# One core: single up products and wide gate pairs in an S4 convolution beside a gated GLU

## The chip, the cores and the metric

One Trainium2 chip, one of its cores. The metric is the device time of one execution in microseconds, lower is better; several runs of each kernel are compared by their medians. TensorE is written PE, VectorE DVE, ScalarE ACT, GpSimd POOL and SyncE SP, as the profile does.

## The reference

The input `A_u` has 2048 tokens of 512 features. It is layer-normalised, and two branches work on the result. The outcome is the input plus both.

```python
x = A_u
xn = _layernorm(x, axis=-1)
# branch A: a diagonal state space model as a long causal convolution, one kernel per feature
P = jnp.exp(logdA[:, :, None] * l[None, None, :])            # logdA = exp(log_dt) * (A_re + 1j A_im), 512 x 128 modes
K = jnp.einsum("dn,dnl,dn->dl", Cc, P, dB).real              # 512 features x 2048 lags
y = irfft(rfft(xn padded) * rfft(K padded))[:L] + xn * Dskip
# branch B: a gated unit with 1792 hidden features
g = xn @ w_gate;  u = xn @ w_up
h = _sigmoid(g) * u
return x + y + h @ w_down
```

## The kernel before, in words

**The parts.** Tokens are loaded (`load_x`, L437) and normalised: statistics L542 and L543, a power on POOL (L492 or L482), normalising L554 (DVE) or L549 (ACT). The first 512 tokens are transposed on PE through `ident` (L565) and copied to `xnT` in two halves, the first by ACT (L572), the second by DVE (L574); the other three groups of 512 tokens go through memory (`x_scr`) and a transposing DMA.

Branch A builds the modes' powers by squaring (L610 to L678), then, for four quarters `c` of 128 features each, two tables G and H by complex products on DVE (`cmul`, L737 to L743, and `squares`, L791 to L797). PE multiplies the tables (`f_k`, L822, 64 small matmuls for each half) to kernel matrices, ACT evicts them to `kq_sb` (L288), they are stored to memory in two pieces (`k_scr`) and reloaded into `kT`; L844 on DVE adds Dskip. Two quarters make one half `pc` of the features. For each half, eight units `u` make the kernel's spectrum on PE (L911), the input's spectrum (L695 to z_scr, then L885), their product on DVE (L916, L920; L898 are copies that swap halves for it) and the way back on PE (L935). Results go through `v_scr` and are reloaded for the last step (L994, L997).

Branch B runs over four groups `grp` of 512 tokens, in each over 14 hidden tiles `k` of 128, taken as seven pairs `u2`. A gate product is four matmuls 128x512 (`fg`, L1045), a sigmoid on ACT puts it into `hT_sb` (L1057, or L1060 for a pair at once), an up product is four matmuls (`fu`, L1069), and DVE multiplies the two. Then the down product (L1123) takes 14 matmuls for each 128 tokens, and ACT evicts it.

**PSUM.** Two pairs of banks (`pair`, pool `s`, 1024 wide) and four single banks (`bank`, pool `gu`). A gate product stands in a single bank; if its pair is listed in `JOINT`, both gate products of the pair stand in one pair of banks and one sigmoid takes 1024 columns.

**Up products.** `UEV` lists the products (number 14 grp + k) whose up part ACT evicts to `us_sb` (L1084). In the kernel before they come in pairs: two evictions fill one of two wide buffers, and one DVE instruction multiplies 128x1024 (L1089). `FLIP` lists the pairs whose second eviction goes first. The other up products are multiplied straight from PSUM, 128x512 (L1094).

**The start of the first group.** For k in `HALF` the gate product is done by halves of its columns, so that it can begin when half of `xnT` is there. Before that PE runs matmuls on a zeroed tile (`keep_warm`, L519).

**The reload of the kernel matrices.** For every quarter two stores and one load of 192 KB; the very last store is issued by ACT, all others by SP.

**What sets the order.** `_Plan.add` records operations in the order of the code; `run` issues them by the list `ORDER`, a written-out permutation of their numbers, and hands out pool slots in that order. Every engine works through its instructions in the order issued, and a DMA waits in its engine's queue until what it needs is done. So one list fixes the order on all five engines, DMAs included.

Of the kernel before, what the change touches and what calls it, by code (L numbers as in the profile page):

```python
# [10 lines left out]
BF = mybir.dt.bfloat16  # L11
# [14 lines left out]
FT = 14  # L26
# [21 lines left out]
FLIP = ((0, 3), (0, 5), (1, 0), (1, 1), (1, 2), (1, 4), (1, 5), (1, 6), (2, 0), (2, 4), (3, 2))  # L48
JOINT = ((0, 2), (0, 3), (0, 5), (0, 6))
# [18 lines left out]
KB = 1024  # L68
# [114 lines left out]
def _consts():  # L183
# [19 lines left out]
UEV = (6, 7, 10, 11, 12, 13, 14, 15, 16, 17, 18, 19, 22, 23, 24, 25, 26, 27, 28, 29, 30, 31, 32, 33, 34, 35, 36, 37, 38, 39, 40, 41, 44, 45, 46, 47, 52, 53, 54, 55,)  # L203
# [115 lines left out]
def kernel(  # L319
# [46 lines left out]
    us_sb = const.tile([128, 2, 2, 512], BF, name="us_sb")  # L366
# [77 lines left out]
    load_x(2, 1)  # L444
    load_x(3, 1)
# [76 lines left out]
    keep_warm(12, -10)  # L522
    for n in (0, 5, 6):
        keep_warm(3 if n < 3 else 1, -9 + n)
# [196 lines left out]
    k_ld = []  # L721
# [27 lines left out]
    for c in range(4):  # L749
# [63 lines left out]
        for half_ in range(2):  # L813
            sl = _Slot("s")

            def f_k(half_=half_, sl=sl, G=G, H=H):
                for y in range(8 * half_, 8 * half_ + 8):
                    pk = bank(sl, y // 4 % 2).rearrange("p (q x) -> p q x", q=4)
                    for comp in range(2):
# [13 lines left out]
        kq_free = [dma("ACT" if cc and c in (3,) else "SP", k_scr[4 * c:4 * c + 4, :, :, cc, :].rearrange("t i h x -> (t i) h x"),  # L833
                       kq[cc:128:2, cc:16:2].rearrange("p h k y -> p h (k y)"), deps=evs, prio=PC, pkt=192)(96 * KB) for cc in range(2)]
        k_st[pc] += kq_free
        half_kT = slice(4 * (c % 2), 4 * (c % 2) + 4)
        k_ld.append(dma("SP", kT[pc][:, half_kT].rearrange("p a c k y -> p a (c k y)"), k_scr[4 * c:4 * c + 4].rearrange("a i h c x -> (i h) a (c x)"),
                        deps=kq_free + W_op + [o_g], prio=PC, pkt=384)(192 * KB))
        if c % 2 == 0:
            continue  # L840

# [3 lines left out]
        kT_op[pc] = [pl.add("DVE", 0.30, f_ds, k_ld[-2:] + [l_dk], PC)]  # L845
# [179 lines left out]
    for grp in range(4):  # L1025
# [5 lines left out]
        for u2 in range(7):  # L1031
# [4 lines left out]
            for k in (2 * u2, 2 * u2 + 1):  # L1036
# [38 lines left out]
                un = FT * grp + k  # L1075
                on = un in UEV

                if on:
                    if k % 2 == 0:
                        eu0, es0 = (b, mu, k), es_  # L1080
                        continue
                    eus, us = [], _Slot("us")
                    for n, (sl, m_, kk) in enumerate([(b, mu, k), eu0] if (grp, u2) in FLIP else [eu0, (b, mu, k)]):
                        eus.append(pl.add("ACT", 0.48, lambda sl=sl, us=us, kk=kk: S.activation(out=us_sb[:, us.idx, kk % 2, :], in_=bank(sl), func=ACT.Identity),  # L1084
                                          [m_] + eus, PSIG, acq=[] if n else [us], rel=[sl], alt=(FT * grp + kk, 1)))

                    def fpd2(hs=hs, us=us):
                        hh = hT_sb[:, hs.idx, :, :].rearrange("p k n -> p (k n)")
                        V.tensor_tensor(out=hh, in0=hh, in1=us_sb[:, us.idx, :, :].rearrange("p k n -> p (k n)"), op=ALU.mult)  # L1089
                    prods.append(pl.add("DVE", 0.33, fpd2, [es0, es_] + eus, PPROD, rel=[us], alt=(un, 2)))  # L1090
                    continue

                def fpd(sl=b, h=h):
                    V.tensor_tensor(out=h(), in0=h(), in1=bank(sl), op=ALU.mult)  # L1094
                tail = dict(rel=[b], alt=(un, 2))
# [117 lines left out]
```

## Time and profile before

| | |
|---|---|
| median of 3 runs | 215.45 us (214.41, 215.45, 215.57) |
| the profiled execution | 215.32 us |
| its span, first to last instruction | 213.4 us |
| granted PE clock, mean | 0.997 |
| DMA moved | 42.61 MB, mean 200 GB/s |

A row of the timeline gives start, length, engine, line, operation, output and inputs, shape, how many in a row, and in brackets the idle time before and what ended it. "q" behind an engine is its sequencer, which issues DMAs. A window row gives the stretch and its length, then busy time and number of instructions on PE, PE's weight loads, DVE, ACT and POOL, the granted PE clock, the DMA engines' busy share and GB/s. Instructions overlap a little with the next one: the distance of two starts is what an instruction costs its engine, its length is more.

### The profile page before, as it was taken

The numbers are of one execution on the slowest core, as the hardware profiler recorded it, in microseconds if no ns is written. First come the engines' busy times: TensorE is split into PE (matmuls) and PEld (weight loads), VectorE is DVE, ScalarE is ACT, GpSimd is POOL, SyncE is SP. The second block draws the span as 40 slices with busy tenths as digits, with TensorE's granted clock in tenths as the row PEclk, the third lists the DMA queues.
The fourth block names the chain that finished last, engine by engine and source line by source line (L and its number), as shares of the span: only waits on it lengthen the run. The fifth ranks groups of instructions, "written<-read, shape, count | busy, mean of one in ns | idle before, by whom it ended". The sixth has DMA issues, their size and how long they took to land.

```text
span 213.4 us, 4897 instructions
## 1 busy us (share of the span) xinstructions
PE 204.0 (96%) x1839; PEld 103.2 (48%) x1864; DVE 191.3 (90%) x406; ACT 176.3 (83%) x284; POOL 33.1 (15%) x40
## 2 busy tenths in 40 slices
PE   7989999999999999999999999999999999999892
PEld 2654444444444454345447464444644655644472
DVE  4799999999999999999999999999973999990494
ACT  4799999999999999998998999779979699960000
POOL 2108030003040000010009970011200000000000
PEclk9999999999999999999999999999999999999998
DMA  5998597013963218788776369589994789897955
GB/s 148 330 372 313 182 225 237 2 52 133 260 139 60 98 55 263 185 238 212 215 216 159 112 174 275 141 231 244 175 257 112 203 252 335 246 288 209 263 195 178
DMA packets 52377, 42.61 MB, mean 200 GB/s; under 512 B 16641, under 2 KB 44546, under 8 KB 52354
## 3 DMA queue, kind: packets, MB, share of 16 engines
q1 hardware_dynamic: 50658, 40.30, 64.3%
q0 software_dynamic: 864, 1.57, 4.8%
q10 hardware_dynamic: 832, 0.43, 0.8%
q8 instruction: 14, 0.23, 0.4%
q14 instruction: 9, 0.07, 0.1%
HBM read 24.99 MB, written 12.85 MB: 177 GB/s over the span
## 4 chain that ended last, share of the span: by engine, by line
PE 59%; ACT 20%; DMA 9%; DVE 6%; issue 4%; POOL 1%; DVEq 0%; ACTq 0%; SPq 0%
PE bank L1069 15%; PE bank L1123 13%; PE bank L1045 11%; PE pair L911 9%; ACT big L288 6%; PE pair L935 5%; ACT hT_sb L1057 3%; PE pair L1045 3%; DMA k_scr<-kq_sb 3%; ACT us_sb L1084 3%; ACT big L669 3%; ACT big L663 2%; DVE big L1020 2%; DMA big<-v_scr 2%; PE pair L822 2%
## 5 line engine op out<-in xcount | busy, mean ns | idle before, releaser
L288 ACT ACTIVATE big<-pair 128x1024 bf16<-128x1024 f32 x64 | 64.6, 1048 | 5.3 <-PE pair L911 2.2
L1069 PE MATMUL bank<-xnT,wu_sb 128*128 128x512 bf16 x212 | 53.0, 379 | 1.1 <-issue 0.6
L1123 PE MATMUL bank<-wd_sb,hT_sb 128*128 128x512 bf16 (+1 forms) x231 | 50.6, 367 | 0.5 <-issue 0.2
L1045 PE MATMUL bank<-xnT,wg_sb 128*128 128x512 bf16 (+1 forms) x194 | 46.6, 370 | 0.5 <-issue 0.3
L1045 PEld LDWEIGHTS <-wg_sb 128*128 128x128 bf16 x240 | 22.7, 98 | 25.8 <-issue 3.0
L1123 PEld LDWEIGHTS <-hT_sb 128*128 128x128 bf16 x238 | 22.4, 98 | 24.9 <-issue 1.9
L1069 PEld LDWEIGHTS <-wu_sb 128*128 128x128 bf16 x224 | 20.7, 98 | 25.5 <-issue 3.4
L1057 ACT ACTIVATE hT_sb<-bank 128x512 bf16<-128x512 f32 x48 | 28.7, 640 | 2.3 <-PE bank L1045 2.3
L737 DVE TENSOR_TENSOR big<-big 128x1024 bf16<-128x1024 bf16 (+4 forms) x40 | 26.8, 670 | 0.2
L738 DVE TENSOR_TENSOR big<-big 128x1024 bf16<-128x1024 bf16 (+4 forms) x40 | 26.6, 666 | 0.0
L1084 ACT ACTIVATE us_sb<-bank 128x512 bf16<-128x512 f32 x40 | 24.7, 640 | 0.0
L911 PE MATMUL pair<-big 128*128 128x256 bf16 x160 | 19.4, 273 | 0.4 <-DVE big L844 0.4
L916 DVE TENSOR_TENSOR big<-big 128x2048 bf16<-128x2048 bf16 x16 | 19.3, 1219 | 0.1
L846 POOL COPY hold<-big 1x1 bf16<-1x1 bf16 x2 | 14.3, 7146 | 30.7 <-DVE big L844 30.7
L911 PEld LDWEIGHTS <-big 128*128 128x128 bf16 x160 | 15.3, 98 | 4.8 <-issue 1.0
L742 DVE TENSOR_TENSOR big<-big 128x512 bf16<-128x512 bf16 (+4 forms) x40 | 16.6, 415 | 0.3
L743 DVE TENSOR_TENSOR big<-big 128x512 bf16<-128x512 bf16 (+4 forms) x40 | 16.6, 414 | 0.0
L791 ACT ACTIVATE sq_sb<-big 128x256 bf16<-128x256 bf16 (+2 forms) x20 | 14.0, 698 | 1.3 <-DVE big L743 1.0
L935 PE MATMUL pair<-big 64*64 64x512 bf16 (+1 forms) x256 | 13.1, 327 | 0.5 <-ACT big L288 0.3
L1089 DVE TENSOR_TENSOR hT_sb<-hT_sb,us_sb 128x1024 bf16<-128x1024 bf16 x20 | 13.5, 684 | 0.0
L288 ACT ACTIVATE big<-big 128x256 bf16<-128x256 bf16 x30 | 13.1, 463 | 0.0
L669 ACT ACTIVATE big<-big 128x1024 f32<-128x1024 f32 x11 | 12.4, 1125 | 0.4 <-DVE big L678 0.4
(100 smaller groups left out, 233.4 us busy)
## 6 DMA issues: line engine op xcount, KB each, us to landing
big<-c_E SPq DMA_DIRECT2D x13, 320.0 KB, 5.1
z_scr<-big SPq DMA_DIRECT2D x16, 256.0 KB, 3.0
big<-z_scr SPq DMA_DIRECT2D x16, 256.0 KB, 3.9
v_scr<-big SPq DMA_DIRECT2D x16, 256.0 KB, 4.1
big<-big SPq DMA_DIRECT2D x44, 64.0 KB, 3.3
big<-in_A_u_dram SPq DMA_DIRECT2D x4, 512.0 KB, 6.7
wu_sb<-in_B_w_up_dram SPq DMA_DIRECT2D x2, 896.0 KB, 10.6
wd_sb<-in_B_w_down_dram SPq DMA_DIRECT2D x1, 1792.0 KB, 8.3
```

What stands on the lines that cost most here:

```text
L288: nc.scalar.activation(out=get(out), in_=get(in_), func=ACT.Identity)
L669: s_op = pl.add("ACT", 0.95, lambda cur=cur, sq=sq: S.activation(out=sq, in_=cur, func=ACT.Square), [cur_op] + W_op[-1:], PLAD + k * 0.01)
L737: V.tensor_tensor(out=wide(outp), in0=wide(lo), in1=mre, op=ALU.mult)
L738: V.tensor_tensor(out=wide(tb()), in0=wide(lo), in1=mim, op=ALU.mult)
L911: T.matmul(two(sk)[:, o:o + DW], es()[:, g, kt, :], kTv[p][:, :, kt, :], start=kt in (0, NKT - 1), stop=kt >= NKT - 2)
L916: V.tensor_tensor(out=pp().rearrange("p q h m -> p (q h) m"), in0=xx().rearrange("p q h m -> p (q h) m"), in1=kb()[:, 0:2 * DW].unsqueeze( ...
L935: T.matmul(two(sv)[o:o + 64, DW * (2 * g + y):2 * DW * (g + 1)], mab[b:b + 64, 2 * u + g, q, :], pq()[b:b + 64, q, ch] if y else pp()[b:b ...
L1045: T.matmul(bank(sl, k % 2)[:, c0:c1], w[:, kt, k * 128:(k + 1) * 128], xnT[:, grp, kt, c0:c1], start=(kt == 0), stop=(kt == KT - 1))
L1057: S.activation(out=hT_sb[:, hs.idx, k % 2, :], in_=bank(sl), func=ACT.Sigmoid)
L1069: T.matmul(bank(sl), wu_sb[:, kt, k * 128:(k + 1) * 128], xnT[:, grp, kt, :], start=(kt == 0), stop=(kt == KT - 1))
L1084: eus.append(pl.add("ACT", 0.48, lambda sl=sl, us=us, kk=kk: S.activation(out=us_sb[:, us.idx, kk % 2, :], in_=bank(sl), func=ACT.Identity ...
L1123: T.matmul(bank(po)[:, 0:c[1] - c[0]], hT_sb[:, hts[k // 2].idx, k % 2, jj * 128:(jj + 1) * 128], wd_sb[:, k, c[0]:c[1]], start=first and ...
```

## The change

- Three pairs of the third group, (2, 1), (2, 3) and (2, 5), join `JOINT`.
- `us_sb` holds single products: two buffers of 512 columns instead of two of 1024. Every product is evicted and multiplied by itself, 128x512. `FLIP` goes. `UEV` lists 40 products, as before, but not the same ones.
- Tokens are loaded as 1, 1, 2 (then 4, 4, 4) instead of 1, 1, 1, 1.
- The reload of the kernel matrices is done once for two quarters, 384 KB, behind all four stores. The last store is issued by SP.
- One more warming call, and 14 instead of 12 matmuls in the first: 22 instead of 17.
- The buffer for POOL's DMA descriptors has the default size.
- `ORDER` is another permutation throughout, since operations are fewer and more: 932 before, 963 after.

```diff
-FLIP = ((0, 3), (0, 5), (1, 0), (1, 1), (1, 2), (1, 4), (1, 5), (1, 6), (2, 0), (2, 4), (3, 2))
-JOINT = ((0, 2), (0, 3), (0, 5), (0, 6))
+JOINT = ((0, 2), (0, 3), (0, 5), (0, 6), (2, 1), (2, 3), (2, 5))
...
-    us_sb = const.tile([128, 2, 2, 512], BF, name="us_sb")
+    us_sb = const.tile([128, 2, 512], BF, name="us_sb")
...
-    load_x(2, 1)
-    load_x(3, 1)
+    load_x(2, 2)
...
-    keep_warm(12, -10)
-    for n in (0, 5, 6):
+    keep_warm(14, -10)
+    for n in (0, 1, 5, 6):
...
-        kq_free = [dma("ACT" if cc and c in (3,) else "SP", k_scr[4 * c:4 * c + 4, :, :, cc, :].rearrange("t i h x -> (t i) h x"),
+        kq_free = [dma("SP", k_scr[4 * c:4 * c + 4, :, :, cc, :].rearrange("t i h x -> (t i) h x"),
...
-        k_ld.append(dma("SP", kT[pc][:, half_kT].rearrange("p a c k y -> p a (c k y)"), k_scr[4 * c:4 * c + 4].rearrange("a i h c x -> (i h) a (c x)"),
-                        deps=kq_free + W_op + [o_g], prio=PC, pkt=384)(192 * KB))
         if c % 2 == 0:
             continue
+        kr = dma("SP", kT[pc].rearrange("p a c k y -> p a (c k y)"), k_scr[8 * pc:8 * pc + 8].rearrange("a i h c x -> (i h) a (c x)"),
+                 deps=k_st[pc] + W_op + [o_g], prio=PC, pkt=384)(384 * KB)
...
-                if on:
-                    if k % 2 == 0:
-                        eu0, es0 = (b, mu, k), es_
-                        continue
...
-                    def fpd2(hs=hs, us=us):
-                        hh = hT_sb[:, hs.idx, :, :].rearrange("p k n -> p (k n)")
-                        V.tensor_tensor(out=hh, in0=hh, in1=us_sb[:, us.idx, :, :].rearrange("p k n -> p (k n)"), op=ALU.mult)
-                    prods.append(pl.add("DVE", 0.33, fpd2, [es0, es_] + eus, PPROD, rel=[us], alt=(un, 2)))
...
+                def feu(sl=b, us=us, on=on):
+                    if on:
+                        S.activation(out=us_sb[:, us.idx, :], in_=bank(sl), func=ACT.Identity)
+                eu = pl.add("ACT", 0.48, feu, [mu], PSIG, acq=[us] if on else [], rel=[b] if on else [], alt=(un, 1))
+
+                def fpd(sl=b, h=h, us=us, on=on):
+                    V.tensor_tensor(out=h(), in0=h(), in1=us_sb[:, us.idx, :] if on else bank(sl), op=ALU.mult)
...
-    nc = _bacc.Bacc("TRN2", target_bir_lowering=False, num_devices=1, dynamic_dma_scratch_size=8192)
+    nc = _bacc.Bacc("TRN2", target_bir_lowering=False, num_devices=1)
```

Two engines in two places, each first before and then in the change. Lines after the changed places have other numbers there: L1083 for L1089 and L1094, L842 for L844, L741 for L742 and so on.

DVE at the start, before, from the statistics of tokens 2 and 3 on (`ln_ve_b`) to the copy into `xnT` and the next statistics:

```order
9 L486 TENSOR_SCALAR ln_ve_b<-mvb 128x2
10 L489 CAST ln_m_f<-mvb 128x2
11 L493 RECIPROCAL ln_ri_f<-ln_sd_b 128x2
12 L554 TENSOR_SCALAR big<-big,ln_m_f,ln_ri_f 128x512 x2
13 L610 TENSOR_TENSOR big<-big 128x512 x2
14 L618 TENSOR_SCALAR big<-big 128x512
15 L619 SCALAR_TENSOR_TENSOR big<-big 128x512
16 L574 COPY xnT<-pair_64 128x4x256
17 L542 BN_STATS stats<-big 128x6 x4
```

DVE in the same place in the change:

```order
10 L610 TENSOR_TENSOR big<-big 128x512
11 L489 CAST ln_m_f<-mvb 128x2
12 L610 TENSOR_TENSOR big<-big 128x512
13 L493 RECIPROCAL ln_ri_f<-ln_sd_b 128x2
14 L554 TENSOR_SCALAR big<-big,ln_m_f,ln_ri_f 128x512
15 L618 TENSOR_SCALAR big<-big 128x512
16 L619 SCALAR_TENSOR_TENSOR big<-big 128x512
17 L554 TENSOR_SCALAR big<-big,ln_m_f,ln_ri_f 128x512
18 L542 BN_STATS stats<-big 128x6 x2
19 L574 COPY xnT<-pair_64 128x4x256
20 L542 BN_STATS stats<-big 128x6
```

Both L610 moved ahead of the normalising of tokens 2 and 3 (L554), which is split, and the first two statistics of tokens 4 to 7 moved ahead of the copy L574.

SP around the last quarter's kernel matrices, before (`big<-big` are the swaps, `big<-z_scr` loads of input spectra, `v_scr` stores of results; the second store of this quarter is in ACT's queue):

```order
73 L422 DMA big<-z_scr 128x4x256
74 L422 DMA big<-big 32x1024
75 L422 DMA big<-z_scr 128x4x256
76 L422 DMA k_scr<-kq_sb 512x1x96
77 L422 DMA big<-c_S 128x128
78 L422 DMA big<-c_SR 128x256
79 L422 DMA big<-big 32x1024 x4
80 L422 DMA big<-k_scr 128x4x192
```

SP in the same place in the change:

```order
74 L423 DMA v_scr_99<-big 128x4x256
75 L423 DMA big<-big 32x1024
76 L423 DMA v_scr_99<-big 128x4x256
77 L423 DMA big<-c_S 128x128
78 L423 DMA k_scr<-kq_sb 512x1x96 x2
79 L423 DMA big<-z_scr 128x4x256
80 L423 DMA big<-big 32x1024 x3
81 L423 DMA big<-k_scr 128x8x192
```

Both stores stand in SP's queue. Of the two z_scr loads ahead of them one has moved behind them and the other to before these rows, with two v_scr stores in between. One swap fewer stands ahead of the reload, and the reload is twice as large.

More of the change, by code (lines that the diff above doesn't have):

```diff
@@ L201, in _consts @@
                 MAB=f(np.stack([quads(MA[by], True), quads(MB[by], True)], axis=2)), E=f(_build_E(M2, by).reshape(128, NU // 2, 2, NKT, 128).transpose(1, 0, 2, 3, 4)))
-UEV = (6, 7, 10, 11, 12, 13, 14, 15, 16, 17, 18, 19, 22, 23, 24, 25, 26, 27, 28, 29, 30, 31, 32, 33, 34, 35, 36, 37, 38, 39, 40, 41, 44, 45, 46, 47, 52, 53, 54, 55,)
+UEV = (0, 6, 7, 9, 11, 12, 13, 14, 15, 16, 17, 18, 19, 21, 23, 24, 25, 26, 28, 29, 30, 31, 32, 33, 34, 35, 36, 37, 38, 39, 40, 41, 43, 44, 46, 47, 49, 52, 54, 55,)
 ON_DVE = (86, 89, 104, 106, 121, 122, 123, 137, 138, 184, 194, 195, 198, 199, 201,)
@@ L720 @@
     kT_op = [[], []]
-    k_ld = []
     k_st = [[], []]
@@ L832 @@
         pc = c // 2
-        kq_free = [dma("ACT" if cc and c in (3,) else "SP", k_scr[4 * c:4 * c + 4, :, :, cc, :].rearrange("t i h x -> (t i) h x"),
+        kq_free = [dma("SP", k_scr[4 * c:4 * c + 4, :, :, cc, :].rearrange("t i h x -> (t i) h x"),
                        kq[cc:128:2, cc:16:2].rearrange("p h k y -> p h (k y)"), deps=evs, prio=PC, pkt=192)(96 * KB) for cc in range(2)]
         k_st[pc] += kq_free
-        half_kT = slice(4 * (c % 2), 4 * (c % 2) + 4)
-        k_ld.append(dma("SP", kT[pc][:, half_kT].rearrange("p a c k y -> p a (c k y)"), k_scr[4 * c:4 * c + 4].rearrange("a i h c x -> (i h) a (c x)"),
-                        deps=kq_free + W_op + [o_g], prio=PC, pkt=384)(192 * KB))
         if c % 2 == 0:
             continue
+        kr = dma("SP", kT[pc].rearrange("p a c k y -> p a (c k y)"), k_scr[8 * pc:8 * pc + 8].rearrange("a i h c x -> (i h) a (c x)"),
+                 deps=k_st[pc] + W_op + [o_g], prio=PC, pkt=384)(384 * KB)
         def f_ds(pc=pc):
@@ L844, in f_ds @@
             V.tensor_tensor(out=kz, in0=kz, in1=dskr[0:1, DW * pc:DW * pc + DW].rearrange("p (a y) -> p a y", y=16), op=ALU.add)
-        kT_op[pc] = [pl.add("DVE", 0.30, f_ds, k_ld[-2:] + [l_dk], PC)]
+        kT_op[pc] = [pl.add("DVE", 0.30, f_ds, [kr, l_dk], PC)]
         pl.add("POOL", 0.1, lambda pc=pc: P.tensor_copy(out=hold[:, pc:pc + 1], in_=kTv[pc][0:1, 0, 0, 0:1]), kT_op[pc], PC)
@@ L1075 @@
                 un = FT * grp + k
+                us = _Slot("us")
                 on = un in UEV
-                if on:
-                    if k % 2 == 0:
-                        eu0, es0 = (b, mu, k), es_
-                        continue
[L1082 to L1085, printed above, removed]
-                    def fpd2(hs=hs, us=us):
-                        hh = hT_sb[:, hs.idx, :, :].rearrange("p k n -> p (k n)")
-                        V.tensor_tensor(out=hh, in0=hh, in1=us_sb[:, us.idx, :, :].rearrange("p k n -> p (k n)"), op=ALU.mult)
-                    prods.append(pl.add("DVE", 0.33, fpd2, [es0, es_] + eus, PPROD, rel=[us], alt=(un, 2)))
[L1091 to L1095, printed above, removed]
+                def feu(sl=b, us=us, on=on):
[4 more added lines that the diff above has]
+                    V.tensor_tensor(out=h(), in0=h(), in1=us_sb[:, us.idx, :] if on else bank(sl), op=ALU.mult)
+                tail = dict(rel=[us] if on else [b], alt=(un, 2))
                 if joint and k % 2 == 0:
-                    held = fpd, [mu], tail
+                    held = fpd, [eu, mu], tail
                     continue
@@ L1100 @@
                     prods.append(pl.add("DVE", 0.33, held[0], held[1] + [es_], PPROD, **held[2]))
-                prods.append(pl.add("DVE", 0.33, fpd, [es_, mu], PPROD, **tail))
+                prods.append(pl.add("DVE", 0.33, fpd, [es_, eu, mu], PPROD, **tail))
         ges = []
```

82 rows, old and new, of the table ORDER are left out of this document.

## Prediction

> **What bounds the kernel now.** I read the page first, for the engines' shares, then the windows by stage, then the timeline where one stage hands over to the next.
>
> ```profile
> PE 204.0 (96%) x1839; PEld 103.2 (48%) x1864; DVE 191.3 (90%) x406; ACT 176.3 (83%) x284; POOL 33.1 (15%) x40
> ```
>
> Three engines are nearly full, so a share alone does not say which one sets the end. The windows do; each row gives the stretch, its length, then busy time by engine:
>
> ```profile
> 0.00:11.70 11.70, 9.45 (x49) 5.00 (x50) 7.40 (x22) 7.36 (x13) 2.32 (x11) 1.00 0.80 252
> 11.70:78.00 66.30, 65.88 (x345) 29.50 (x354) 66.04 (x156) 65.77 (x111) 11.41 (x16) 1.00 0.56 165
> 78.00:154.00 76.00, 75.05 (x850) 38.45 (x860) 75.43 (x163) 70.43 (x122) 18.90 (x12) 1.00 0.75 197
> 154.00:165.80 11.80, 10.83 (x207) 5.25 (x208) 6.72 (x12) 10.47 (x14) 0.00 (x0) 1.00 0.73 188
> 165.80:191.00 25.20, 24.75 (x252) 14.40 (x256) 24.82 (x43) 21.38 (x27) 0.43 (x1) 1.00 0.89 264
> 191.00:213.40 22.40, 18.00 (x143) 10.56 (x143) 10.85 (x14) 0.90 (x2) 0.00 (x0) 0.97 0.71 217
> ```
>
> From 11.7 to 154 VectorE rests 0.83 us in all and TensorE 1.37 us. Both are bounds, at the full granted clock (1.00): VectorE makes the long-convolution kernel's factors, TensorE fills the time with gate, up and down products. From 154 to 165.8 VectorE is busy for 6.72 of 11.80 us. That is the handover: the last quarter of the kernel matrices goes through memory.
>
> ```profile
> 154.02 1.40 PEld L822 LDWEIGHTS <-big 128*32 128x32 bf16 x128 [0.42 <-DVE big L743]
> 154.03 1.53 PE L822 MATMUL pair<-big 128*32 128x82 bf16 x128
> 155.02 1.51 ACT L288 ACTIVATE kq_sb<-pair 128x768 bf16<-128x768 f32 x2 [0.53 <-PE pair L822]
> 156.56 0.64 ACTq L422 DMA_DIRECT2D k_scr<-kq_sb  x1
> 156.63 0.57 SPq L422 DMA_DIRECT2D k_scr<-kq_sb  x1
> 158.44 3.68 SPq L422 DMA_DIRECT2D big<-big  x4
> 162.74 0.38 SPq L422 DMA_DIRECT2D big<-k_scr  x1
> 165.49 0.28 DVE L844 TENSOR_TENSOR big<-big,dskr 1x256 bf16<-1x256 bf16 x1 [0.51 <-DMA big<-k_scr]
> 165.82 2.36 PE L911 MATMUL pair<-big 128*128 128x256 bf16 x20 [0.35 <-DVE big L844]
> ```
>
> The last kernel matmuls (L822, 154.03) wait for VectorE's last factor; their result is evicted, stored, reloaded, corrected by L844, and the second half's spectra (L911) start at 165.82. What starts later there ends later, because TensorE is busy for 24.75 of the next 25.20 us.
>
> **The change part by part.** The sum is made against the profiled execution: 215.32 us, its span 213.4; the median of the runs is 215.45.
>
> *Products one by one.* 20 wide products, 128x1024, become 40 of 128x512. Four of the narrow form on VectorE run from the first row below to the start of the second; two wide ones follow them:
>
> ```profile
> 52.16 0.41 DVE L742 TENSOR_TENSOR big<-big 128x512 bf16<-128x512 bf16 x1
> ...
> 53.51 1.21 DVE L737 TENSOR_TENSOR big<-big 128x2048 bf16<-128x2048 bf16 x1
> ...
> 189.28 1.29 DVE L1089 TENSOR_TENSOR hT_sb<-hT_sb,us_sb 128x1024 bf16<-128x1024 bf16 x2
> 190.48 1.88 DVE L1094 TENSOR_TENSOR hT_sb<-hT_sb,bank 128x512 bf16<-128x512 bf16 x3
> ```
>
> A narrow one steps in 1.35/4 = 0.34 us, a wide one in 1.20/2 = 0.60. A pair costs 2 x 0.3375 - 0.60 = 0.075 more. Ahead of the last kernel factor the old order has 16 wide products and the new 32 narrow ones, with the same other work (ten products straight from PSUM in both). So VectorE gets 16 x 0.075 = 1.2 us more there; with whole durations instead of steps (2 x 0.41 - 0.645) it would be 2.8, the upper bound. The four remaining pairs cost 0.3 after 154, beside its idle time there.
>
> [...]
>
> *The start.* The new order puts two token statistics (L542) ahead of the copy L574, which hands the second half of the first transposed tokens to TensorE, and both L610 ahead of the normalising of tokens 2 and 3.
>
> ```profile
> 0.73 1.81 SPq L422 DMA_DIRECT2D big<-in_A_u_dram  x4
> ...
> 4.02 0.51 SPq L422 DMA_DIRECT2D big<-in_A_u_dram  x1
> ...
> 6.65 0.63 ACT L608 ACTIVATE big<-big 128x512 bf16<-128x512 bf16 x1 [0.40 <-DMA big<-in_A_par_dram]
> ...
> 7.47 1.02 ACT L572 ACTIVATE xnT<-pair 128x1024 bf16<-128x1024 bf16 x1 [0.20 <-PE pair L565]
> ...
> 10.40 0.69 DVE L619 SCALAR_TENSOR_TENSOR big<-big 128x512 f32<-128x512 f32 x1
> ...
> 11.01 0.69 DVE L574 COPY xnT<-pair 128x1024 bf16<-128x1024 bf16 x1
> ...
> 11.61 2.46 DVE L542 BATCH_NORM_STATS2 stats<-big 128x6 f32<-128x512 bf16 x4
> ...
> 11.75 0.60 PE L1045 MATMUL pair<-xnT,wg_sb 128*128 128x256 bf16 x4 [0.85 <-DVE xnT L574]
> ```
>
> ```profile
> L422 SPq DMA_DIRECT2D big<-in_A_u_dram x1: 505/505/505, 4.0 to 4.0; - x1
> ...
> DMA to landing us min/median/max: 6.8/6.8/6.8
> ```
>
> Tokens 4 to 7 (issued 4.02) land 6.8 us later, at 10.8. In the new order their load stays the eighth transfer of SP's queue (one token load fewer, the small dskr load ahead instead) with the same bytes ahead, so I keep 10.8. Then two statistics (2.46/4 = 0.6 each) end at 12.0 and L574 at 12.7: the second halves of the gates start 0.95 later. VectorE itself is not behind: at 12.7 it has done 1.2 us more than it had at 11.7, a lead of 0.25 (from -0.3 to +1.2: the latter if the tokens came before it asks, near 9.7). On ScalarE L615 now stands ahead of L572 and waits for the first L610, which waits for L608 (done at 7.28); with 0.6 to 0.7 for each of the two, as L619 takes, L572 moves from 7.47 to about 8.6. Five more warming matmuls fill that wait, and the first gate halves and transposes still end near 12.0, ahead of 12.7: no price of their own.
>
> *The kernel path.* VectorE's last factor is ready 1.2 - 0.25 = 0.95 us later. TensorE comes there with four 128x512 matmuls fewer done (counted in the two orders, warming left out):
>
> ```profile
> 168.18 0.86 PE bank L1069 x4
> 169.04 0.34 PE pair L885 x4
> ```
>
> so at 154.03 + 0.95 - 0.86 = 154.1 at the earliest, while VectorE is ready near 155.0. VectorE decides, and the late gates cost nothing more. Behind the last kernel matmuls the new order has those four matmuls (0.86) more to fill the wait and four small ones (0.34) fewer. At the first L911 of the second half TensorE has therefore 0.3 us more left than before.
>
> The reload is now one of 384 KB for both quarters, where the last one carried 192. Rows of nearby sizes, KB and us to landing:
>
> ```profile
> big<-c_E SPq DMA_DIRECT2D x13, 320.0 KB, 5.1
> ...
> big<-v_scr SPq DMA_DIRECT2D x4, 384.0 KB, 7.2
> ...
> big<-k_scr SPq DMA_DIRECT2D x4, 192.0 KB, 5.0
> ```
>
> Against 5.0 that is 0.1 to 2.2 more; I take 1.0, as 192 KB at the 188 GB/s of the window 154:165.8. The second store moves from ACT's queue to SP's, behind the first: 0.6 (156.63 row). Against it, of the two 256 KB spectrum loads issued just ahead of the stores one now follows them and the other is issued well before; each would be 1.36 at that rate, so between 0 and 2.7 go. I take 1.1, less than one of them, for v_scr stores, swaps and the k_scr stores still share the engines. Net 0.5, from -1.5 to +2.2.
>
> *The rest.* Three pairs evicted wide instead of six narrow sigmoids:
>
> ```profile
> L1057 ACT ACTIVATE hT_sb<-bank 128x512 bf16<-128x512 f32 x48 | 28.7, 640 | 2.3 <-PE bank L1045 2.3
> L1060 ACT ACTIVATE hT_sb<-pair 128x1024 bf16<-128x1024 f32 x4 | 4.1, 1052 | 0.0
> ```
>
> 6 x 0.60 - 3 x 1.03 = 0.5 us less on ScalarE, which has 5.6 us to spare from 78 to 154: nothing. It holds while ScalarE is not last. From 165.8 on, both orders hold the same work in nearly the same places, and the last products wait for the same reload from v_scr. Nothing.
>
> Sum: 0.95 (factors) + 0.5 (store and reload) + 0.3 (work left) = 1.75; 215.32 + 1.75 = 217.1 us.
>
> **Rivals.** *No change, 215.8.* Tokens 4 to 7 land by 10.0, as one transfer fewer is queued ahead. L574 then ends at 11.9, VectorE's lead is about 1.0 and cancels the 1.2; the 0.5 is covered by the four further matmuls, and the 0.3 stays: 215.32 + 0.2 + 0.3 = 215.8. For it: SP's first four loads take 1.81 us to issue, 0.45 each. Against it: 252 GB/s in 0:11.7, so the bytes ahead and not the issues set the landing.
>
> *Faster, 213.9.* TensorE alone is the bound and the new order packs it better. From 11.7 to 191 it rests 0.42 + 0.95 + 0.97 + 0.45 = 2.8 us; with half of that gone, 215.32 - 1.4 = 213.9. For it: four more matmuls in the longest rest, 0.5 us less on ScalarE. Against it: VectorE has 0.57 us free of 76.00 and gets more work. It decides if the last kernel matmuls start before 153.
>
> *Much slower, 218.7.* The us buffer holds two single products instead of two pairs. ScalarE's eviction then waits until VectorE has multiplied the one two before, and behind that stand ScalarE's spectrum evictions, for which TensorE's PSUM pairs wait. If a quarter of the 40 evictions wait 0.3 us and half of that is hidden, the forecast grows by 1.5 or so, to 218.7. For it: a VectorE without rest multiplies late. Against it: ScalarE's 5.6 us.
>
> **How the numbers follow.** No measurement here tells less than 0.5%, 1.08 us, from no change: 214.37 to 216.53. Forecast 0.52, of which 0.08 falls inside that band (a lighter reload); no change 0.26; faster 0.12; much slower 0.10. Slower: 0.44 + 0.10 = 0.54; same 0.08 + 0.26 = 0.34; faster 0.12. The range goes from no change with the lightest kernel path (215.8 - 1.5 = 214.3) to the forecast with the heaviest reload (217.1 + 2.2 = 219.3); the faster case stays outside. Alone, the forecast spans 216.0 to 219.3.
>
> **What would show it.** Right: L574 ends near 12.7 after a wait for tokens; the last kernel matmuls start near 155 and wait for VectorE; L844's successor near 167; a VectorE without rest from 13 to 155. Wrong: those matmuls start by 154, or they wait for TensorE's own queue or ScalarE; a us eviction that idles for VectorE; the reload landing within 3 us.

## The result, and the profile after

The changed kernel takes 221.38 us, the median of four runs (220.87 to 223.39); the kernel before, beside it, 215.12. The ratio is 1.031, 95% interval 1.024 to 1.039: slower by 6.3 us between the medians, 6.7 by the ratio. The forecast was 217.1, at most 219.3. The profiled execution took 221.72 us, its span 219.7. Every ratio below is against the kernel before, run beside it (medians 214.33 to 215.15 us). All times are medians of runs in the faster of two states; one run of 220.50 us in the slower state, of the kernel with halves at the end of experiment 9, is left out.

The page's first line, and the waits that are new, from the waits by engine:

```profile
PE 208.2 (95%) x1869; PEld 104.8 (48%) x1869; DVE 192.9 (88%) x426; ACT 176.9 (81%) x281; POOL 51.8 (24%) x40
```

```profile
PE pair L821 <- POOL big L770: 3.4, 1, 3.4
...
DVE big L736 <- ACT big L289: 3.6, 1, 3.6
...
DVE ln_ri_f L501 <- POOL ln_sd_b L482: 0.9, 1, 0.9
...
ACT us_sb L1079 <- DVE hT_sb L1083: 0.2, 1, 0.2
```

VectorE's busy time is 1.6 us more, but its share fell, and POOL's time grew from 33.1 to 51.8. The third quarter's kernel matmuls (L821) on TensorE waited 3.4 us for two small memsets on POOL. The last row is the forecast's much slower rival, ScalarE's eviction waiting for a product: 0.2 us, once.

The timeline of the changed kernel at that place: POOL's copy of one element into `hold`, what stands behind it, TensorE, and VectorE on both sides of its rest.

```profile
112.14 0.27 DVE L842 TENSOR_TENSOR big<-big,dskr 1x256 bf16<-1x256 bf16 x1
...
112.48 19.72 POOL L844 COPY hold<-big 1x1 bf16<-1x1 bf16 x1 [17.74 <-DVE big L842]
...
127.10 0.67 DVE L737 TENSOR_TENSOR big<-big 128x1024 bf16<-128x1024 bf16 x1
...
127.70 0.41 DVE L1083 TENSOR_TENSOR hT_sb<-hT_sb,us_sb 128x512 bf16<-128x512 bf16 x1
...
128.04 0.41 DVE L741 TENSOR_TENSOR big<-big 128x512 bf16<-128x512 bf16 x1
...
131.74 0.41 DVE L737 TENSOR_TENSOR big<-big 128x512 bf16<-128x512 bf16 x1
132.14 0.20 POOL L770 MEMSET big<- 128x128 bf16 x1
...
132.39 2.09 PE L821 MATMUL pair<-big 128*32 128x82 bf16 x128 [3.39 <-POOL big L770]
...
135.72 0.39 DVE L736 TENSOR_TENSOR big<-big 128x256 bf16<-128x256 bf16 x1 [3.57 <-ACT big L289]
```

One element is copied in 19.7 us. No other line of the kernel reads `hold`; the copy only makes POOL's queue wait for L842. The copy ends in the moment in which VectorE has nothing left to do (132.15), and VectorE has nothing left because ScalarE waits for TensorE, TensorE for the memsets, and the memsets for the copy ahead of them in POOL's queue. In the kernel before the same copy was there too:

```profile
112.35 13.86 POOL L846 COPY hold<-big 1x1 bf16<-1x1 bf16 x1 [17.35 <-DVE big L844]
...
125.49 0.67 DVE L738 TENSOR_TENSOR big<-big 128x1024 bf16<-128x1024 bf16 x1
...
126.16 0.20 POOL L771 MEMSET big<- 128x128 bf16 x1
126.19 0.43 DVE L742 TENSOR_TENSOR big<-big 128x512 bf16<-128x512 bf16 x1
...
127.30 0.80 PE L822 MATMUL pair<-big 128*32 128x82 bf16 x64
```

There it took 13.9 us and was over 1.1 us before L822 began. It ended where VectorE paused: L738 is over at 126.16, L742 begins at 126.19, while most of VectorE's instructions begin some 0.07 us before the last one ends. L742 is the second half of a complex product and needs what L738, its first half, has just written. In the change a product (L1083, 127.70) stands between the two halves, and from 101.6 to 132.1 VectorE has no pause at all.

The handover of the changed kernel:

```profile
160.38 1.28 PEld L821 LDWEIGHTS <-big 128*32 128x32 bf16 x128 [0.42 <-DVE big L742]
160.39 1.42 PE L821 MATMUL pair<-big 128*32 128x82 bf16 x128
...
167.22 0.52 SPq L423 DMA_DIRECT2D big<-k_scr  x1
...
171.40 0.27 DVE L842 TENSOR_TENSOR big<-big,dskr 1x256 bf16<-1x256 bf16 x1
...
171.73 2.35 PE L909 MATMUL pair<-big 128*128 128x256 bf16 x20
```

The last kernel matmuls wait for VectorE's last factor (L742) and start 6.36 us later than before (154.03). From there to the second half it takes 11.34 us (before 11.79), from there to the end 47.99 (before 213.41 - 165.82 = 47.59). So the whole loss lies ahead of 160.39.

### The profile page after: what moved, and what is told of

It reads as the page before. It is cut to its first block, busy times and chain, and to the rows that moved or that the text cites. A ratio compares the mean times of both kernels' runs of the same rounds, so it can differ in the third digit from the quotient of the medians.

```text
span 219.7 us, 4936 instructions
## 1 busy us (share of the span) xinstructions
PE 208.2 (95%) x1869; PEld 104.8 (48%) x1869; DVE 192.9 (88%) x426; ACT 176.9 (81%) x281; POOL 51.8 (24%) x40
## 4 chain that ended last, share of the span: by engine, by line
PE 44%; DVE 25%; issue 13%; DMA 7%; ACT 4%; POOL 4%; SPq 1%; DVEq 0%; POOLq 0%; ACTq 0%
PE bank L1112 15%; PE bank L1043 8%; PE bank L1067 7%; DVE hT_sb L1083 4%; PE pair L909 4%; PE pair L933 4%; DMA big<-in_A_u_dram 3%; POOL ln_sd_b L482 3%; PE pair L1043 2%; DVE big L736 2%; DVE big L737 2%; DMA big<-k_scr 2%; DVE big L678 2%; DVE stats L542 2%; ACT big L289 2%
## 5 line engine op out<-in xcount | busy, mean ns | idle before, releaser
L1067 PE MATMUL bank<-xnT,wu_sb 128*128 128x512 bf16 x224 | 54.2, 379 | 0.6 <-DVE hT_sb L1083 0.6
L1043 PE MATMUL bank<-xnT,wg_sb 128*128 128x512 bf16 (+1 forms) x176 | 42.1, 375 | 0.9 <-ACT xnT L572 0.8
L844 POOL COPY hold<-big 1x1 bf16<-1x1 bf16 x2 | 20.0, 10017 | 31.1 <-DVE big L842 31.1
L737 DVE TENSOR_TENSOR big<-big 128x1024 bf16<-128x1024 bf16 (+4 forms) x40 | 26.4, 661 | 0.0
L1055 ACT ACTIVATE hT_sb<-bank 128x512 bf16<-128x512 f32 x42 | 24.5, 616 | 1.8 <-PE bank L1043 1.8
L1079 ACT ACTIVATE us_sb<-bank 128x512 bf16<-128x512 f32 x40 | 24.1, 615 | 1.1 <-PE bank L1067 0.9
L1083 DVE TENSOR_TENSOR hT_sb<-hT_sb,us_sb 128x512 bf16<-128x512 bf16 x40 | 16.4, 413 | 2.6 <-ACT us_sb L1079 1.3
L909 PEld LDWEIGHTS <-big 128*128 128x128 bf16 x160 | 15.4, 98 | 5.0 <-issue 1.8
L741 DVE TENSOR_TENSOR big<-big 128x512 bf16<-128x512 bf16 (+4 forms) x40 | 16.4, 411 | 0.2
L742 DVE TENSOR_TENSOR big<-big 128x512 bf16<-128x512 bf16 (+4 forms) x40 | 16.4, 411 | 0.0
L1043 PE MATMUL pair<-xnT,wg_sb 128*128 128x512 bf16 (+1 forms) x64 | 14.4, 353 | 0.6 <-DVE xnT L574 0.6
L790 ACT ACTIVATE sq_sb<-big 128x256 bf16<-128x256 bf16 (+2 forms) x20 | 13.3, 663 | 1.1 <-DVE big L742 1.1
L542 DVE BATCH_NORM_STATS2 stats<-big 128x6 f32<-128x512 bf16 x15 | 10.0, 687 | 3.6 <-DMA big<-in_A_u_dram 3.6
```

The source lines that it names most:

```text
L737: V.tensor_tensor(out=wide(tb()), in0=wide(lo), in1=mim, op=ALU.mult)
L844: pl.add("POOL", 0.1, lambda pc=pc: P.tensor_copy(out=hold[:, pc:pc + 1], in_=kTv[pc][0:1, 0, 0, 0:1]), kT_op[pc], PC)
L909: T.matmul(two(sk)[:, o:o + DW], es()[:, g, kt, :], kTv[p][:, :, kt, :], start=kt in (0, NKT - 1), stop=kt >= NKT - 2)
L1043: T.matmul(bank(sl, k % 2)[:, c0:c1], w[:, kt, k * 128:(k + 1) * 128], xnT[:, grp, kt, c0:c1], start=(kt == 0), stop=(kt == KT - 1))
L1055: S.activation(out=hT_sb[:, hs.idx, k % 2, :], in_=bank(sl), func=ACT.Sigmoid)
L1067: T.matmul(bank(sl), wu_sb[:, kt, k * 128:(k + 1) * 128], xnT[:, grp, kt, :], start=(kt == 0), stop=(kt == KT - 1))
```

## The experiments

**Theory.** POOL's copy does not end while VectorE runs its instructions without a pause (19.7 us, to 132.15); what queues behind it reaches TensorE late. **Rivals.** VectorE's own extra work is what is late; or POOL's copy is slow for another reason; or the further narrow instructions cost the time by themselves.

**1. The copy moved away.** In the changed kernel, POOL's copy goes behind the other memsets, ahead of the second such copy:

```diff
 L1149 DMA glu_sb<-in_A_u_dram 128x1024
-L844 COPY hold<-big 1x1
 L770 MEMSET big 128x64x2
 ...
-L844 COPY hold<-big 1x1
+L844 COPY hold<-big 1x1 x2
```

> The changed kernel with one instruction moved: GpSimd's 1x1 copy into hold (L844, first half) goes behind the memsets of the third and fourth quarter. Theory (GpSimd shut out): that copy, 19.7 us long, ends only when VectorE runs dry, the memsets L770 and L771 stand behind it, the third quarter's kernel matmuls (L821) wait 3.4 us for them, then VectorE rests 3.6 us behind ScalarE. Without it L821 starts at 129.0 to 129.5 instead of 132.4, VectorE's rest of 3.57 is gone, and the time falls from 221.4 by 3.6 to 4.8: 216.6 to 217.8 us. Rival (VectorE's own extra work is what is late, the wait only fills it): the wait moves to VectorE, less than 1 us is gained, 220.4 or more.

217.93 us, 1.014 of before (1.010 to 1.018), where the change had 1.031; 0.1 us above the range expected. L821 starts with no wait for POOL:

```profile
128.67 1.41 PE L821 MATMUL pair<-big 128*32 128x82 bf16 x128
```

The moved copy still took 2.9 us (from 152.56) and ended as VectorE ran dry (155.37), where nothing waited for it. The last kernel matmuls start at 155.23, not 160.39. More than half of the loss goes with this wait.

**2. The same move in the kernel before**, as a control.

> The kernel before with the same move, as a control. Theory: its copy of 13.9 us ended at 126.2 and the third quarter's kernel matmuls came at 127.3, so nothing waited: no change, 214.6 to 215.7 us. Rival (the copy itself slows VectorE or another engine while it lasts): faster by 1 us or more.

215.37 us, ratio 1.000 (0.998 to 1.003). The copy costs nothing where it ends in time.

**3. One exchange on VectorE.** In the changed kernel the product at 127.70 goes behind the second half of the complex product:

```diff
 L736 TENSOR_TENSOR big<-big 128x128x8
 L737 TENSOR_TENSOR big<-big 128x1024
-L1083 TENSOR_TENSOR hT_sb<-hT_sb,us_sb 128x512
 L741 TENSOR_TENSOR big<-big 128x64x8
 L742 TENSOR_TENSOR big<-big 128x64x8
+L1083 TENSOR_TENSOR hT_sb<-hT_sb,us_sb 128x512
```

> The changed kernel with two neighbours on VectorE exchanged: one product (L1083, at 127.70) goes behind the second half of the complex product (L741, L742) that it had split from its first half (L736, L737). Theory: the second half then stands directly behind the first, whose result it needs, VectorE pauses for 34 ns near 127.7, GpSimd's copy into hold ends there instead of at 132.2, the memsets follow at 128.0, L821 starts near 129.3 and the time is that of the kernel with the copy moved away, 217.4 to 218.5 us. Rival (the copy needs something else than a pause, or the wait is long by chance): it still ends near 132, and the time is 220.9 to 221.9.

218.10 us, ratio 1.016 (1.013 to 1.019). Same work, same copy in the same place of POOL's queue:

```profile
112.11 15.35 POOL L844 COPY hold<-big 1x1 bf16<-1x1 bf16 x1 [17.74 <-DMA big<-big]
...
126.74 0.67 DVE L737 TENSOR_TENSOR big<-big 128x1024 bf16<-128x1024 bf16 x1
...
127.40 0.21 POOL L770 MEMSET big<- 128x128 bf16 x1
127.44 0.43 DVE L741 TENSOR_TENSOR big<-big 128x512 bf16<-128x512 bf16 x1
...
128.56 1.42 PE L821 MATMUL pair<-big 128*32 128x82 bf16 x128
```

L737 ends at 127.41, L741 begins at 127.44, and there the copy ends: by its row at 127.46, while the memset behind it starts at 127.40 already. Two neighbours exchanged are worth 3.3 us (1.031 to 1.016).

**4. The reverse: the pause of the kernel before, filled.** One multiplication that nothing needs stands between the two halves at 125.49 and 126.19, in three forms.

```diff
         def f_b():
+            if at_b == 319:
+                V.tensor_tensor(out=fill[:], in0=wd_sb[:, 0, :], in1=wd_sb[:, 1, :], op=ALU.mult)
```

First 128x128, `ident` by itself:

> The kernel before with one instruction more on VectorE: a product of 128x128 that nothing needs, between the two halves of the complex product at 125.49 and 126.19, where VectorE paused for 34 ns and GpSimd's copy into hold ended. Theory: the pause is filled, the copy runs on until VectorE is dry or reads PSUM, the memsets L771 and L772 come late, the third quarter's kernel matmuls (L822, 127.30) wait, and the time rises by 2 to 4 us, to 217.2 to 219.2. Rival (one small instruction more, 0.15 us, and nothing else): 215.0 to 215.6.

214.80 us, 1.002 (1.000 to 1.003): the expectation failed. The copy ended at 126.72, right behind the filler. Then 128x128 of two different tiles:

> The kernel before with the filling instruction again, but its two operands are two different tiles (ident and a piece of wd_sb, 128x128), where the first one multiplied ident by itself and the copy into hold still ended right behind it, at 126.72. If a full pause is what GpSimd needs and the first filler failed because it read one tile twice: the copy runs on past 127.5 and the time rises to 217 to 219 us. If any short instruction there does as well: the copy ends near 126.7 again, 214.6 to 215.4.

214.67 us, 1.001 (0.999 to 1.003), the copy ended at 126.3. Then the size of a product, as in the diff:

> As the last, with a filler of the products' own size, 128x512 from two pieces of wd_sb (0.34 us). In the changed kernel a product of that size in that place did keep the copy waiting. Theory: the copy runs on past 127.5, L822 waits for the memsets, 217.3 to 219.3 us. Rival (in the kernel before something else lets the copy end at 126.2 to 126.7): 215.2 to 215.9 us.

220.43 us, 1.028 (1.024 to 1.032): one instruction of 0.34 us more, and 6.0 us lost, more than the 3 to 5 expected. Its timeline:

```profile
112.15 18.77 POOL L850 COPY hold<-big 1x1 bf16<-1x1 bf16 x1 [17.32 <-DVE big L848]
...
125.29 0.67 DVE L738 TENSOR_TENSOR big<-big 128x1024 bf16<-128x1024 bf16 x1
...
125.89 0.41 DVE L744 TENSOR_TENSOR fill<-wd_sb 128x512 bf16<-128x512 bf16 x1
...
126.22 0.41 DVE L746 TENSOR_TENSOR big<-big 128x512 bf16<-128x512 bf16 x1
...
130.87 0.21 POOL L775 MEMSET big<- 128x128 bf16 x1
...
131.12 1.36 PE L826 MATMUL pair<-big 128*32 128x82 bf16 x64 [3.94 <-POOL big L775]
...
136.64 0.40 DVE L737 TENSOR_TENSOR big<-big 128x256 bf16<-128x256 bf16 x1 [5.77 <-ACT big L288]
```

That is the changed kernel's fault, made in the kernel before by one instruction. With the second short filler:

```profile
125.47 0.67 DVE L738 TENSOR_TENSOR big<-big 128x1024 bf16<-128x1024 bf16 x1
...
126.07 0.21 DVE L744 TENSOR_TENSOR fill<-ident,wd_sb 128x128 bf16<-128x128 bf16 x1
126.20 0.41 DVE L746 TENSOR_TENSOR big<-big 128x512 bf16<-128x512 bf16 x1
...
126.27 0.21 POOL L775 MEMSET big<- 128x128 bf16 x1
```

The short filler starts 0.07 us before L738 ends, and the second half, which needs L738's result, starts at 126.20, behind L738's end at 126.14. With this filler, a step of 0.13 us, the copy ended there; with one of 0.34 us it ran on to 130.9. That VectorE pauses behind the short filler, though its rows show no pause, is argued from these rows, not shown.

**5. Small instructions put where the copy waits.** In the changed kernel, behind three products, to see whether the copy ends at one of them:

```diff
+                    if un == 36:
+                        V.memset(door[:, 0:1], 0.0)
+                    if un == 41:
+                        V.reciprocal(out=door[:, 1:2], in_=one[:])
+                    if un == 39:
+                        V.bn_stats(out=door[:, 2:8], in_=h())
```

> The changed kernel with three small instructions on VectorE added behind products, while GpSimd's copy into hold waits (112.5 to 132.1): a memset of one column near 113.4, a reciprocal of one column from memory near 118.3, statistics of 128x512 near 121.5. [...] Rival (the copy is slow by itself or waits for something else): it still ends near 132 and the time stays at 221 to 222.5.

219.34 us, 1.020 (1.014 to 1.025): faster than the change, but above the 217 to 218.5 us expected if the copy ended at one of the three, and its four runs lie far apart (218.10 to 220.14). The products come in another order than the expectation took: the memset stood at 120.68, the reciprocal at 125.64, the statistics at 127.94. The copy ran on through the first two, which began before the instruction ahead had ended. It ended at 127.96, at the pause of 0.03 us ahead of the statistics, which read what the product before them had written. Another kernel had the first filler of experiment 4 (`ident` by itself) behind the product at 120.3:

> The changed kernel with the same small instruction as in the first filling (ident by itself, 128x128) added behind the product at 120.3, while the copy into hold waits. If that instruction lets GpSimd in: the copy ends near 120.8 and the time falls to 217.7 to 218.7 us. If not, because it was the wait of the second half behind it that did so: the copy ends near 132 and the time stays at 221 to 222.

222.27 us, 1.035 (1.031 to 1.039); the copy ended at 131.43 with VectorE dry. The copy did not end at the filler by itself, which leaves the waiting second half as what let it end in experiment 4.

**6. The second wait for POOL.** At 45.86 POOL's power (L482) of the last tokens took 6.49 us, and VectorE's L501 waited 0.89 for it. Here a second half is issued directly behind its own first half as well:

```diff
 L737 TENSOR_TENSOR big<-big 128x512
-L741 TENSOR_TENSOR big<-big 128x64x8
-L742 TENSOR_TENSOR big<-big 128x64x8
-L1083 TENSOR_TENSOR hT_sb<-hT_sb,us_sb 128x512
 L741 TENSOR_TENSOR big<-big 128x64x4
 L742 TENSOR_TENSOR big<-big 128x64x4
+L741 TENSOR_TENSOR big<-big 128x64x8
+L742 TENSOR_TENSOR big<-big 128x64x8
+L1083 TENSOR_TENSOR hT_sb<-hT_sb,us_sb 128x512
```

> As the exchange of the product, and one more: at 47.7 to 49 the second half (L741, L742, 256 columns) of a complex product is issued directly behind its first half instead of behind another second half and a product. Theory: that makes a pause near 47.7, GpSimd's power (L482, 45.86 to 52.35) ends there, L501 no longer waits 0.89 us for it, and the time is 0.5 to 0.9 lower than with the one exchange: 216.6 to 217.6 us. Rival (VectorE's 0.89 us are covered later, or the power needs more than one pause): the same time as with the one exchange.

217.06 us, 1.012 (1.010 to 1.013), about 0.9 us less than with one exchange, though the two intervals overlap a little. The pause is at 47.63 to 47.66:

```profile
45.72 2.81 POOL L482 TENSOR_TENSOR ln_sd_b<-ln_ve_b,half 128x4 bf16<-128x4 bf16 x1
...
47.21 0.42 DVE L737 TENSOR_TENSOR big<-big 128x512 bf16<-128x512 bf16 x1
...
47.66 0.29 DVE L741 TENSOR_TENSOR big<-big 128x256 bf16<-128x256 bf16 x1
...
51.41 0.16 DVE L501 RECIPROCAL ln_ri_f<-ln_sd_b 128x4 f32<-128x4 bf16 x1
```

The power takes 2.81 us instead of 6.49, and L501 follows its neighbours at once. Its row ends at 48.53, 0.87 us behind the pause; in the changed kernel it ended 0.86 us behind the moment in which VectorE ran dry (51.49). Both times the power ended some 0.87 us behind VectorE's pause, not at it.

**7. The narrow products alone**, in the kernel before:

```diff
-V.tensor_tensor(out=hh, in0=hh, in1=us_sb[:, us.idx, :, :]..., op=ALU.mult)
+[V.tensor_tensor(out=hh[:, q:q + 512], in0=hh[:, q:q + 512], in1=us_sb[:, us.idx, q // 512, :], op=ALU.mult) for q in (0, 512)]
```

> The kernel before with each of its 20 wide products as two instructions of 128x512, all else in the same order. By the steps in the changed kernel (32 narrow ones 10.67 us, the 16 wide ones of before 9.95) VectorE gets 0.7 to 0.9 us more ahead of the last factor: 215.8 to 216.3 us. If the 34 ns gap of VectorE at 126.16, in which the copy into hold ended, closes by it, the copy runs on until VectorE is dry and the kernel matmuls wait: 3 to 4 us more, 219 to 220. [...]

216.37 us, 1.005 (1.002 to 1.008): 1.1 us by the ratio. The pause stayed and the copy ended in it. Over 20 further instructions that is 0.055 us each (0.03 to 0.08 by the interval), an estimate from the time as a whole.

**8. The reload by halves alone**, in the kernel before. The empty operation on SP stands in for the load that is gone:

```diff
-kq_free = [dma("ACT" if cc and c in (3,) else "SP", k_scr...
+kq_free = [dma("SP", k_scr...
-k_ld.append(dma("SP", kT[pc][:, half_kT]..., k_scr[4 * c:4 * c + 4]...)(192 * KB))
 if c % 2 == 0:
+    pl.add("SP", 0.0, lambda: None, kq_free + W_op + [o_g], PC)
     continue
+k_ld.append(dma("SP", kT[pc]..., k_scr[8 * pc:8 * pc + 8]..., deps=k_st[pc] + W_op + [o_g])(384 * KB))
```

> The kernel before with the reload of the kernel matrices as in the change, one load of 384 KB for two quarters, and the very last store issued by SP. The prediction's term: 0.4 to 1.6 us more between the last kernel matmuls and the second half's first spectrum (11.8 us), of it 0.6 for the store and 0.1 to 2.2 for the larger load: 215.6 to 216.7 us. By the changed kernel's trace, where that stretch took 11.3 us: no change, 214.6 to 215.6. Rival: gain of over 0.5, because the third quarter's own load no longer shares the engines.

215.71 us, 1.006 (1.004 to 1.007): 1.1 us between the medians. The load is issued at 161.99 and L845, which is L844 in the kernel before, starts 4.3 us later; before it was 2.8 us (162.74 to 165.49):

```profile
161.99 0.53 SPq L422 DMA_DIRECT2D big<-k_scr  x1
...
166.30 0.28 DVE L845 TENSOR_TENSOR big<-big,dskr 1x256 bf16<-1x256 bf16 x1 [1.93 <-DMA big<-k_scr]
...
166.64 1.05 PE L912 MATMUL pair<-big 128*128 128x256 bf16 x8 [1.78 <-DVE big L845]
```

**9. What remains in the changed kernel.** Both exchanges, and the reload by quarters again:

```diff
+L423 DMA big<-k_scr 128x4x192
 ...
 L423 DMA k_scr<-kq_sb 512x1x96 x2
 ...
-L423 DMA big<-k_scr 128x8x192
+L423 DMA big<-k_scr 128x4x192
```

> The changed kernel with both exchanges on VectorE, and the kernel matrices reloaded by quarters as before (192 KB each, the third quarter's load ahead of time), its last store still on SP. Theory (the halves cost what they cost in the kernel before, 1.1 us): 1.1 us less than with the exchanges alone, 1.1% over the kernel before: 215.5 to 216.5 us, of it some 1.1 us for the narrow products. Rival (the load's size is hidden behind TensorE's work): the same 216.8 to 217.4 as without it.

217.16 us, 1.014 (1.010 to 1.018): no gain. In the kernel with both exchanges L842 stands on VectorE behind a product that waits 1.34 us for its eviction. Next that product goes behind L842, with halves and with quarters:

```diff
-L1083 TENSOR_TENSOR hT_sb<-hT_sb,us_sb 128x512
 L842 TENSOR_TENSOR big<-big,dskr 1x16x16
-L1083 TENSOR_TENSOR hT_sb<-hT_sb,us_sb 128x512
+L1083 TENSOR_TENSOR hT_sb<-hT_sb,us_sb 128x512 x2
```

> The changed kernel with both exchanges, and L842 (the Dskip row) moved ahead of the one product on VectorE that stood before it and waited 1.34 us for its eviction, while the reload had landed at 166.42. Theory (VectorE's order holds the second half back): L842 starts near 166.5 instead of 167.06, 0.3 to 0.6 us less than with the exchanges alone: 216.4 to 216.8 us. Rival (TensorE's own work in that stretch sets the start of the second half): the same, 217.0 to 217.4.

> The same with the reload by quarters, whose last load landed at 165.81 without any gain. Theory (the gain was hidden behind that product's wait): L842 near 166.0, 0.9 to 1.3 us less than with quarters alone, 215.8 to 216.3 us; what is then left against the kernel before, 1.1 to 1.6 us, is that of the narrow products. Rival (TensorE's own work sets it): 216.9 to 217.4.

216.91 us, 1.011 (1.009 to 1.014), and 216.84, 1.011 (1.009 to 1.014). Neither moves the time beyond its interval. With quarters:

```profile
163.73 0.28 DVE L844 TENSOR_TENSOR big<-big,dskr 1x256 bf16<-1x256 bf16 x1
163.76 1.89 PE L1045 MATMUL bank<-xnT,wg_sb 128*128 128x512 bf16 x8
...
165.48 2.35 PE L911 MATMUL pair<-big 128*128 128x256 bf16 x20
```

The matrices are there at 164.0, and TensorE has eight gate matmuls to do first, until 165.5: its own order holds the start of the second half. Of the three explanations, the size of the load, VectorE's order and TensorE's own work, the last is the one that is left for this start. It does not explain the time. With quarters the second half starts 11.26 us behind the last kernel matmuls (154.22), with halves and the same order 12.77, and still the times are alike. Behind that start the run with quarters takes 49.08 us, where experiment 6 takes 48.24. What takes the gain back is not shown.

## Why the prediction was wrong

**The step that failed** is the term for the factors on the kernel path: "VectorE's last factor is ready 1.2 - 0.25 = 0.95 us later". VectorE did decide, as forecast: the last kernel matmuls waited for its last factor. But they came 6.4 us later instead of 0.95. The term counts only VectorE's own work and takes for granted that VectorE does not rest. From 11.7 us to the last kernel matmuls its work was 1.3 us more than before (busy 142.75 us against 141.47), while its rest grew from 0.9 us to 5.9. Of this 3.6 and 0.9 are the two waits behind POOL. What had changed is where VectorE pauses: the copy ended at the pause of 126.16 before, and in the change at 132.15, when VectorE had run dry. POOL was read as 15% busy and left out, though the profile of before had the sign in its list of groups:

```profile
L846 POOL COPY hold<-big 1x1 bf16<-1x1 bf16 x2 | 14.3, 7146 | 30.7 <-DVE big L844 30.7
```

```profile
165.83 0.43 POOL L846 COPY hold<-big 1x1 bf16<-1x1 bf16 x1 [13.30 <-DVE big L844]
```

An instruction that moves one element and takes 7 us on average is waiting: the second of the two took 0.43 us, beside copies on VectorE with one operand (L898). Behind the first in POOL's queue stood memsets that TensorE needs, with less than 1.1 us to spare. Nothing in the prediction asked how long that would stay so.

**Factors, 0.95 forecast.** With both waits for POOL gone (experiment 6) the last kernel matmuls start at 154.71, 0.68 later than before. That this is near 0.95 is partly luck, for two errors cancel. The products were forecast at 1.2; in experiment 6 VectorE is busy 0.73 us longer up to there (142.20 against 141.47), while experiment 7 measured 1.1 (0.5 to 1.6) for all 20 pairs in the order of before. The lead of 0.25 from the start did not come: with the same work done, VectorE reached L502 at 18.86 before, at 19.09 in the change and at 18.95 in experiment 6. L574 ended at 13.12, not 12.7, behind tokens waited for until 11.24.

The prediction's upper bound for the products, 2.8, was misread: it took half of 1.29 us for one wide product, but 1.29 spans two that overlap. The profile before gives 684 ns for one (L1089), which makes it 2.2.

**Store and reload, 0.5 forecast, -1.5 to +2.2.** The parts that it was made of, 0.1 to 2.2 and 0.6, less 0 to 2.7, give -2.0 to +2.8. In the kernel before, with the spectrum loads left where they were, store and load cost 1.1. In the changed one the stretch took 11.34 us, less than before; with the waits gone it took 167.38 - 154.71 = 12.67, 0.88 more, by these rows of experiment 6:

```profile
154.71 0.98 PE L821 MATMUL pair<-big 128*32 128x82 bf16 x77
...
167.38 1.36 PE L909 MATMUL pair<-big 128*128 128x256 bf16 x11
```

There TensorE's own order sets the start of the second half (experiment 9), so this says little about the reload.

**Work left on TensorE, 0.3 forecast.** From 167.38 to the end it takes 48.24 us, 0.65 more than before; in the changed kernel itself it is 0.40 (47.99).

The three are stretches of one execution, so they sum to what its span is longer, 2.2 us, where 1.75 was forecast; by the ratio of all its runs, 1.012, it is about 2.5 us. So without POOL's waits the time would have lain in the forecast's range; the rest of the loss, some 4.2 us, goes with the two waits. **The rivals:** the much slower one had the sign, but its mechanism is worth 0.2 us. The two that began at TensorE or the tokens did not show.

Left open: how the 2.2 to 2.5 us that remain divide between the narrow products and TensorE's order. Wide products in the new order were not tried.

## What to carry to other kernels

Where a nearly full VectorE and a nearly idle GpSimd share a kernel, look up every GpSimd instruction whose duration is out of all proportion to its size (here one element in 13.9 us), and then what stands behind it in its queue and when that is needed (here memsets, with less than 1.1 us to spare). Here the new order of VectorE filled the pause of 0.03 us at which the copy had ended. Placing the copy behind what others wait for took the ratio from 1.031 to 1.014 (experiment 1) and cost nothing in the kernel before (1.000, experiment 2); a dependent pair of VectorE instructions put side by side took it to 1.016 (experiment 3), and two such pairs to 1.012 (experiment 6).

## What the runs showed of the hardware

- GpSimd's copy of one element took 13.9, 15.4, 18.8 and 19.7 us, through 23 to 41 whole instructions of VectorE, all with two operands in memory. It ended at a pause of VectorE of 0.03 us or more; with the short fillers it ended without a pause in the rows, as argued in experiment 4. In the kernel before, the two memsets behind the copy, which read nothing, took 0.20 and 0.21 us (126.16 and 126.30), the second beside a VectorE at work.
- In the changed kernel a conversion on POOL took 8.98 us and ended at 68.66, 0.13 us after the first product straight from PSUM since its start had begun. In the traces of its eight variants the conversion ends 0.12 to 0.16 us behind that product's start too. That the product let it end is not shown, as no run moved the product:

```profile
59.68 8.98 POOL L709 CAST pre<-xnT 128x4 f32<-128x4 bf16 x1
```

```profile
68.53 0.67 DVE L1083 TENSOR_TENSOR hT_sb<-hT_sb,bank 128x512 bf16<-128x512 bf16 x1
```

- Not all of it fits: in the kernel before L482 passed in 1.33 us at 50.60 with no pause in VectorE's rows, and it did so in all its variants. That stays open.
- TensorE's rest of 3.4 us was followed by a lower clock. The windows of the changed kernel, around it and after it:

```profile
129.00:132.40 3.40, 0.01 (x3) 0.03 (x3) 3.14 (x9) 1.17 (x3) 3.40 (x3) 1.00 0.85 220
132.40:138.00 5.60, 5.60 (x156) 3.13 (x156) 2.28 (x8) 3.15 (x5) 0.09 (x1) 0.70 0.57 157
```

The granted clock was 0.70 over the next 5.6 us, and four gate matmuls took 1.89 us (at 134.42) in place of 1.04 (at 147.07). The mean granted clock was 0.983 to 0.992 in every run of the three kernels with such a rest (the change, the third filler of experiment 4, the second kernel of experiment 5), and 0.995 or more in all other runs counted here.
